# Sliding-window attention with a gated feed-forward layer: a shorter tail ahead of a branch that is jumped over

## The chip, the cores and the metric

The kernel runs on one core of a Trainium2 chip. The metric is the device time of one execution in microseconds (us); the kernel before was run three times, and the median counts. One further execution was taken with the hardware profiler, and all rows of the profile come from that one.

## What is computed

The input is one sequence of 2048 tokens with 448 features in bf16. Both halves of the layer start from the same normalised input, and their results are added to the input:

```python
xn = _layernorm(x)                                  # x is [1, 2048, 448]
# A: 16 heads of 28 features, causal window of W = 256 keys
scores = einsum("bhqd,bhkd->bhqk", q, k) * (Dh ** -0.5)
mask = (idx[:, None] - idx[None, :] >= 0) & (idx[:, None] - idx[None, :] < W)
p = softmax(where(mask, scores, -1e9))
A = (p @ v) @ wo
# B: gated feed-forward layer with 1792 hidden features
B = (gelu(xn @ w_gate) * (xn @ w_up)) @ w_down
return x + A + B
```

## The kernel before

The tokens are cut into four blocks of 512 queries (`qb`), each of four tiles of 128 rows. For each block the kernel computes scores, `Exp`, the product with the values, the gate and up projections with the Gelu, and then the down projection together with the product with `wo` (`gen_down`, L392), to which VectorE adds the input (L382, tile `res`). SyncE sends each finished tile of 128 rows to the output (L385). A plan written out by hand sets the order: the matmuls of one block are laid between the attention steps of another, so TensorE is kept busy almost without a gap. The last block has no attention step behind it, so the kernel ends with its down projection; its last tile is cut into two halves of 224 columns, and the second half (tile `pl`) is the last thing that TensorE computes.

The softmax subtracts no maximum. That is safe only while the sums of the exponentials stay in a sensible range. Near the end VectorE therefore looks at all reciprocals of these sums (`inv_all`, between `INV_LO` = 1e-18 and `INV_HI` = 1e18), reduces the answer to one integer, `flag`, and every engine loads it into a register (L889, `n_ok`). Behind the last piece of the down projection each engine compares and branches (L899): if `n_ok` is below 1, it falls through into `general_path`, which computes everything again with a maximum subtracted; otherwise it jumps over it. A hint at the head of the program tells VectorE and TensorE that this branch is likely taken; the other three engines have no hint.

Between the last residual and the branch stand three small operations that compute nothing that is used: a copy by Pool (GpSimd) of half a tile of the last `res` into `g2` (L892), a second copy by Pool of that into `g1` (L893), and VectorE's memset of one column of `g1` (L894). Since each reads or overwrites what the one ahead has written, VectorE reaches its branch only when both copies are done.

Two things about the end are not in the source and come from how the program is built. First, transfers that SyncE starts signal their landing on eight semaphores in turn, called lanes here (lane 0 to lane 7); the last output transfer is on lane 7. Second, code behind the branch counts on the same semaphore values whichever way was taken. So the side on which `general_path` is jumped over holds, for each engine, one instruction that waits until its own semaphore has its value and adds what the general path would have added; on SyncE there is one such compensating wait for each lane that the general path uses. They carry the line of the `If`, L899. Behind it stands the common end (L1020): SyncE waits for the eight lanes in order, 0 to 7, each wait paired with a second semaphore. The pair of the sixth is VectorE's count, that of the seventh TensorE's, that of the eighth ScalarE's. Then it drains, and the five engines meet in a barrier that Pool gathers, twice.

In the general path the kernel before starts 24 transfers: for each `qb` two that swap the partition halves of `xnT` into `xsw`, and one for each of the 16 tiles of the output. They use all eight lanes, three to a lane.

Of the kernel before, what the change touches and what calls it, by code (L numbers as in the profile page):

```python
# [10 lines left out]
ALU = mybir.AluOpType  # L11
AX = mybir.AxisListType
bf16 = mybir.dt.bfloat16
f32 = mybir.dt.float32
i32 = mybir.dt.int32

S, D, H, Dh, F = 2048, 448, 16, 28, 1792
P = 128
NT = S // P
NF = F // P  # L20
QB, NB = 512, 4
# [6 lines left out]
def kernel(  # L28
# [11 lines left out]
    nc = tc.nc  # L40
# [19 lines left out]
    outv = out.rearrange("b (n p) d -> p (b n) d", p=P)  # L60


    x_sb = const.tile([P, NT, D], bf16, name="x_sb")
# [36 lines left out]
    ident = const.tile([P, P], bf16, name="ident")  # L100
# [36 lines left out]
    xnT = const.tile([P, 4, S], bf16, name="xnT")  # L137
    xsw = const.tile([P, 3, 2 * QB], bf16, name="xsw")
# [205 lines left out]
    last_res = []  # L344
# [526 lines left out]
    g1 = work.tile([P, 512], f32, name="g1", tag="wc", bufs=2)  # L871
    g2 = work.tile([P, 512], f32, name="g2", tag="wb", bufs=1)
# [16 lines left out]
    n_ok = nc.values_load(flag[0:1, 0:1], min_val=0, max_val=1)  # L889
    for _ in last:  # L890
        pass
    nc.gpsimd.tensor_copy(out=g2[:, 0:D // 2], in_=last_res.pop()[:, 0:D // 2])  # L892
    nc.gpsimd.tensor_copy(out=g1[:, 0:D // 2], in_=g2[:, 0:D // 2])  # L893
    nc.vector.memset(g1[:, 0:1], 0.0)  # L894
    phase[0].close()
    fast.close()
# [7 lines left out]
def general_path(tc, locals_):  # L904

    nc = tc.nc
    L = locals_
    x_sb, xnT, qT, kT, v_sb, wd, wo, ident = (L[k] for k in ("x_sb", "xnT", "qT", "kT", "v_sb", "wd", "wo", "ident"))
    with ExitStack() as st:
        keep = st.enter_context(tc.tile_pool(name="gkeep", bufs=1))  # L910
        wk = st.enter_context(tc.tile_pool(name="gwork", bufs=2))
        ps = st.enter_context(tc.tile_pool(name="gpsum", bufs=1, space=bass.MemoryType.PSUM))
        NEG = -1e37
        mask = keep.tile([P, 3 * P], f32, name="gmask")
        nc.gpsimd.memset(mask[:, :], 0.0)
        nc.gpsimd.affine_select(out=mask[:, :], in_=mask[:, :], pattern=[[1, 3 * P]], compare_op=ALU.is_ge, fill=NEG,
                                base=-1, channel_multiplier=-1)
        nc.gpsimd.affine_select(out=mask[:, :], in_=mask[:, :], pattern=[[-1, 3 * P]], compare_op=ALU.is_ge, fill=NEG,
                                base=256, channel_multiplier=1)
        hT = keep.tile([P, NF, QB], bf16, name="ghT")  # L920
        for qb in range(NB):
            ts = slice(qb * QB, (qb + 1) * QB)
            for hi in range(2):
                nc.sync.dma_start(out=L["xsw"][64 * hi:64 * hi + 64, :, 0:QB], in_=xnT[64 - 64 * hi:P - 64 * hi, 0:3, ts])
            for f in range(NF):
                hi, p = divmod(f, 7)
                r = slice(64 * hi, 64 * hi + 64)
                pg = ps.tile([P, QB], f32, name="pg", tag="pg")
                pu = ps.tile([P, QB], f32, name="pu", tag="pu")
                for dst, w in ((pg, L["wg"]), (pu, L["wu"])):  # L930
                    for c in range(7):
                        x = xnT[r, 3, ts] if c == 6 else xnT[r, c // 2, ts] if c % 2 == hi else L["xsw"][r, c // 2, 0:QB]
                        nc.tensor.matmul(dst[:, :], lhsT=w[r, c, p * P:(p + 1) * P], rhs=x, start=(c == 0), stop=(c == 6),
                                         tile_position=(64 * hi, 0))
                ge = wk.tile([P, QB], bf16, name="gge")
                nc.scalar.activation(out=ge[:, :], in_=pg[:, :], func=ACT.Gelu_apprx_tanh)
                nc.vector.tensor_tensor(out=hT[:, f, :], in0=ge[:, :], in1=pu[:, :], op=ALU.mult)
            for g in range(4):
                pg = ps.tile([P, QB], f32, name="pg", tag="pg")
                for c in range(4):  # L940
                    n, w = (64, L["w3p"]) if c == 3 else (P, L["wqp"][:, c, :, :])
                    nc.tensor.matmul(pg[:, :], lhsT=w[0:n, 4 * g:4 * g + 4, :].rearrange("p h d -> p (h d)"), rhs=xnT[0:n, c, ts],
                                     start=(c == 0), stop=(c == 3))
                nc.vector.tensor_copy(out=qT[:, g, 0:QB], in_=pg[:, :])
            for tt in range(4):
                qt = 4 * qb + tt
                kt0 = max(0, qt - 2)
                nk = qt - kt0 + 1
                w = nk * P
                o_sb = wk.tile([P, H, 32], bf16, name="go")  # L950
                nc.vector.memset(o_sb[:, :, :], 0.0)
                for h in range(H):
                    g, r = h // 4, slice(32 * (h % 4), 32 * (h % 4) + Dh)
                    sc = ps.tile([P, 3 * P], f32, name="gsc", tag="sc")
                    nc.tensor.matmul(sc[:, 0:w], lhsT=qT[r, g, tt * P:(tt + 1) * P], rhs=kT[r, g, kt0 * P:(qt + 1) * P],
                                     start=True, stop=True, tile_position=(32 * (h % 4), 0))
                    sm = wk.tile([P, 3 * P], f32, name="gsm")
                    nc.vector.tensor_tensor(out=sm[:, 0:w], in0=sc[:, 0:w], in1=mask[:, 3 * P - w:3 * P], op=ALU.add)
                    mx = wk.tile([P, 1], f32, name="gmx")
                    nc.vector.reduce_max(out=mx[:, :], in_=sm[:, 0:w], axis=AX.X)  # L960
                    dm = wk.tile([P, 3 * P], f32, name="gdm")
                    nc.vector.tensor_scalar(out=dm[:, 0:w], in0=sm[:, 0:w], scalar1=mx[:, 0:1], scalar2=None, op0=ALU.subtract)
                    pr = wk.tile([P, 3 * P], bf16, name="gpr")
                    rs = wk.tile([P, 1], f32, name="grs")
                    nc.scalar.activation(out=pr[:, 0:w], in_=dm[:, 0:w], func=ACT.Exp, scale=SCALE, accum_out=rs[:, 0:1])
                    pT = ps.tile([P, 3, P], bf16, name="gpT", tag="pT")
                    for b in range(nk):
                        nc.tensor.transpose(out=pT[:, b, :], in_=pr[:, b * P:(b + 1) * P], identity=ident[:, :])
                    pTs = wk.tile([P, 3, P], bf16, name="gpTs")
                    nc.vector.tensor_copy(out=pTs[:, 0:nk, :], in_=pT[:, 0:nk, :])  # L970
                    ov = ps.tile([P, 32], f32, name="gov", tag="ov")
                    for b in range(nk):
                        nc.tensor.matmul(ov[:, :], lhsT=pTs[:, b, :], rhs=v_sb[:, kt0 + b, h, :], start=(b == 0), stop=(b == nk - 1))
                    ri = wk.tile([P, 1], f32, name="gri")
                    nc.vector.reciprocal(out=ri[:, :], in_=rs[:, :])
                    nc.vector.tensor_scalar(out=o_sb[:, h, 0:Dh], in0=ov[:, 0:Dh], scalar1=ri[:, 0:1], scalar2=None, op0=ALU.mult)
                for j, (t0, n) in enumerate(SLOTS):
                    c = 4 * (t0 % 7)
                    nc.vector.tensor_copy(out=o_sb[:, j:j + 4 * n - 3:4, Dh:32],
                                          in_=o_sb[:, 14 + t0 // 7, c:c + 4 * n].rearrange("p (g i) -> p g i", i=4))  # L980
                nc.vector.memset(o_sb[:, 14:16, :], 0.0)
                oT = ps.tile([P, 4, P], bf16, name="goT", tag="oT")
                for g in range(4):
                    nc.tensor.transpose(out=oT[:, g, :], in_=o_sb[:, 4 * g:4 * g + 4, :].rearrange("p h d -> p (h d)"), identity=ident[:, :])
                oTs = wk.tile([P, 4, P], bf16, name="goTs")
                nc.vector.tensor_copy(out=oTs[:, :, :], in_=oT[:, :, :])
                po = ps.tile([P, D], f32, name="gpo", tag="po")
                for g in range(4):
                    nc.tensor.matmul(po[:, :], lhsT=oTs[:, g, :], rhs=wo[:, g, :], start=(g == 0), stop=False)
                for f in range(NF):  # L990
                    nc.tensor.matmul(po[:, :], lhsT=hT[:, f, tt * P:(tt + 1) * P], rhs=wd[:, f, :], start=False, stop=(f == NF - 1))
                res = wk.tile([P, D], bf16, name="gres")
                nc.vector.tensor_tensor(out=res[:, :], in0=po[:, :], in1=x_sb[:, qt, :], op=ALU.add)
                nc.sync.dma_start(out=L["outv"][:, qt, :], in_=res[:, :])


# [28 lines left out]
```

## Time and profile before

| what | us |
|---|---|
| median of 3 runs | 214.26 |
| lowest, highest | 214.17, 214.38 |
| the profiled execution's own time | 214.34 |
| span of its instructions in the profile | 212.6 |
| the execution's time outside that span | 1.74 |

The profile is a page of views: busy time of each engine, the span in 40 slices, the DMA queues, the chain of work that ended last, and the costliest groups. Further answers of the same trace list instructions in order of time (the timeline), or all instructions of one source line. In such a list for one line a row reads: line, engine, operation, count, then the shortest, the median and the longest duration in ns, then the start of the first and of the last in us from the span's start. An engine's name with a q (SPq, DVEq) is its sequencer, which issues, waits and branches.

### The profile page before, as it was taken

What the parts mean: (1) busy time and instruction counts of PE and PEld (TensorE: products, weight loads), DVE (VectorE), ACT (ScalarE), POOL (GpSimd) and SP (SyncE); (2) the same over time, 40 slices, a digit from 0 to 9 for tenths busy, and PEclk for the clock granted to TensorE, in tenths of its full rate; (3) what the DMA queues carried; (4) which work ended last, traced back from release to release, by engine and by line L of the source; (5) the groups of instructions that cost most, each with busy time, mean ns of one, the idle gap of its engine ahead of it and who ended that gap; (6) DMA issues with size and microseconds to landing.
All of it is one profiled execution on the core that took longest, in us unless ns stands there. A gap on an engine that the chain in (4) does not pass through costs nothing.

```text
span 212.6 us, 6354 instructions
## 1 busy us (share of the span) xinstructions
PE 207.7 (98%) x2686; PEld 97.8 (46%) x2686; DVE 157.4 (74%) x355; ACT 131.6 (62%) x123; POOL 48.8 (23%) x86
## 2 busy tenths in 40 slices
PE   7999999999999999999999999999999999999993
PEld 2433444444444445444445444544444454544662
DVE  7799998999767985696537897395384798569622
ACT  4689578565777977413777787532576886656000
POOL 5287658442000220041000102023000022006001
PEclk9999999999999999999999999999999999999999
DMA  6999679978420101003421000100000001000011
GB/s 191 276 218 222 99 194 230 230 217 180 105 51 27 43 3 41 10 1 70 74 74 46 25 0 27 22 0 25 22 3 0 25 26 42 6 3 0 23 59 39
DMA packets 23993, 15.67 MB, mean 74 GB/s; under 512 B 9208, under 2 KB 23832, under 8 KB 23960
## 3 DMA queue, kind: packets, MB, share of 16 engines
q1 hardware_dynamic: 22918, 14.87, 30.4%
q8 instruction: 22, 0.36, 0.7%
q10 hardware_dynamic: 1042, 0.34, 0.7%
q14 instruction: 11, 0.09, 0.1%
HBM read 9.26 MB, written 2.41 MB: 55 GB/s over the span
## 4 chain that ended last, share of the span: by engine, by line
PE 97%; ACT 1%; issue 1%; DVE 0%; DVEq 0%; ACTq 0%
PE po L392 24%; PE gt L458 20%; PE u L458 12%; PE ue L458 8%; PE pq L334 7%; PE sc L654 6%; PE ov L626 5%; PE pv L320 4%; PE wps L150 2%; PE pq L191 2%; PE pl L392 2%; PE pv L191 1%; ACT p_sb L658 1%; PE s L191 1%; PE pk L191 1%
## 5 line engine op out<-in xcount | busy, mean ns | idle before, releaser
L658 ACT ACTIVATE p_sb<-sc 128x2048 bf16<-128x2048 f32 x39 | 73.2, 1878 | 20.5 <-PE sc L654 13.5
L498 ACT ACTIVATE p_sb<-gt 128x1024 bf16<-128x1024 f32 x28 | 28.7, 1024 | 33.7 <-PE gt L458 30.7
L593 POOL TENSOR_TENSOR oN<-oc,l 128x512 bf16<-128x512 f32 x16 | 21.6, 1356 | 119.9 <-DVE l L606 119.9
L458 PE MATMUL gt<-xnT,wg 64*128 64x512 bf16 x224 | 45.6, 376 | 0.0
L392 PE MATMUL po<-wd,hT 128*128 128x448 bf16 x210 | 43.3, 353 | 0.0
L458 PE MATMUL gt<-xsw,wg 64*128 64x512 bf16 x168 | 40.7, 376 | 0.0
L506 DVE TENSOR_TENSOR hT<-p_sb,u 128x512 bf16<-128x512 bf16 x34 | 21.9, 677 | 16.0 <-PE u L458 15.8
L574 DVE TENSOR_TENSOR p_sb<-p_sb,masks 128x256 bf16<-128x256 bf16 (+1 forms) x90 | 27.8, 363 | 7.6 <-ACT p_sb L658 7.6
L392 PEld LDWEIGHTS <-hT 128*128 128x128 bf16 x238 | 21.9, 98 | 19.4 <-issue 2.2
L458 PEld LDWEIGHTS <-wg 64*128 64x128 bf16 x392 | 19.0, 94 | 22.5 <-issue 0.2
L458 PEld LDWEIGHTS <-wu 64*128 64x128 bf16 x392 | 18.6, 94 | 22.5 <-issue 0.8
L458 PE MATMUL u<-xnT,wu 64*128 64x512 bf16 x136 | 28.1, 376 | 0.0
L458 PE MATMUL u<-xsw,wu 64*128 64x512 bf16 x102 | 24.7, 376 | 0.0
L458 PE MATMUL ue<-xnT,wu 64*128 64x512 bf16 x88 | 18.0, 377 | 0.0
L382 DVE TENSOR_TENSOR res<-po,x_sb 128x448 bf16<-128x448 f32 x15 | 9.0, 619 | 11.5 <-PE po L392 11.0
L654 PE MATMUL sc<-qT,kT 28*64 28x320 bf16 (+7 forms) x648 | 16.4, 261 | 0.1
L458 PE MATMUL ue<-xsw,wu 64*128 64x512 bf16 x66 | 16.4, 377 | 0.0
L584 POOL TENSOR_SCALAR_AFFINE_SELECT p_sb<-p_sb 128x512 bf16<-128x512 bf16 (+1 forms) x21 | 14.2, 701 | 6.6 <-ACT p_sb L658 6.5
L611 DVE TENSOR_TENSOR oc<-oc,ov 128x512 f32<-128x512 f32 x12 | 8.2, 681 | 8.7 <-ACT oc L610 8.7
L654 PEld LDWEIGHTS <-kT 28*64 28x64 bf16 (+1 forms) x648 | 7.5, 102 | 13.3 <-issue 12.0
L475 DVE CAST hT<-ue 128x512 bf16<-128x512 f32 x18 | 11.6, 680 | 1.9 <-PE ue L458 1.8
L392 PE MATMUL po<-wo,oN 128*128 128x448 bf16 x54 | 12.0, 352 | 0.0
(111 smaller groups left out, 281.8 us busy)
## 6 DMA issues: line engine op xcount, KB each, us to landing
out_dram<-res SPq DMA_DIRECT2D x15, 112.0 KB
x_sb<-in_A_x_dram SPq DMA_DIRECT2D x3, 448.0 KB
wd<-in_B_w_down_dram SPq DMA_DIRECT2D x3, 448.0 KB
xsw<-xnT SPq DMA_DIRECT2D x6, 192.0 KB
wu<-in_B_w_up_dram SPq DMA_DIRECT2D x2, 560.0 KB
wg<-in_B_w_gate_dram SPq DMA_DIRECT2D x2, 448.0 KB
wg<-in_B_w_gate_dram SPq DMA_DIRECT2D x2, 336.0 KB
wraw<-in_A_wqkv_dram SPq DMA_DIRECT2D x2, 252.0 KB
```

The source lines that it names most:

```text
L334: nc.tensor.matmul(ps, lhsT=w.rearrange("p h d -> p (h d)"), rhs=xchunk(qb, hi, c, qb * QB, QB), start=c == 0, stop=c == 6, tile_position= ...
L392: nc.tensor.matmul(po[:, 0:w], lhsT=x[:, k, tt * P:(tt + 1) * P], rhs=wt[:, k, lo:up], start=start and n == 0, stop=stop and n == len(term ...
L458: nc.tensor.matmul(ps, lhsT=w[64 * hi:64 * hi + 64, c, p * P:(p + 1) * P], rhs=xchunk(qb, hi, c, qb * QB, QB), start=c == 0, stop=c == 6, ...
L475: copy(out=hTs[qb][:, p + 7 * i, :], in_=us[i])
L498: nc.scalar.activation(out=ges[p][:, :, :], in_=gt[:, :, :], func=ACT.Gelu_apprx_tanh)
L506: nc.vector.tensor_tensor(out=hT[:, p + 7 * i, :], in0=ge[:, i, :], in1=u, op=ALU.mult)
L574: nc.vector.tensor_tensor(out=reg, in0=reg, in1=m, op=ALU.mult)
L584: nc.gpsimd.affine_select(out=reg, in_=reg, pattern=mid + [[1 if diag else -1, min(w, P)]], compare_op=ALU.is_ge, fill=0.0, base=0 if diag ...
L593: nc.gpsimd.tensor_tensor(out=oN[:, g, :], in0=oc[:, :], in1=inv, op=ALU.mult)
L626: nc.tensor.matmul(ov[half or 0][32 * j:32 * j + 32, q0:q0 + nq], lhsT=v_sb[r, kt, 4 * g + j, :], rhs=p_sb[r, j, col:col + nq], start=n == ...
L654: nc.tensor.matmul(ss[k0:k0 + nk, j, col:col + nq], lhsT=kT[r, g, kt * P + k0:kt * P + k0 + nk], rhs=qT[r, g, ring(qb).start + q0:ring(qb) ...
L658: nc.scalar.activation(out=p_sb[:, :, 0:ncol], in_=ss[:, :, 0:ncol], func=ACT.Exp, scale=SCALE)
```

## The change

The general path now makes the swapped halves by matmuls with a permutation (`gswap`), copied by VectorE into `xsw`; it adds the residual in place into `x_sb`, and sends the whole output with one transfer at its end. So it starts one transfer, on lane 0, where it started 24. Ahead of the branch one copy by Pool goes: Pool copies the half tile of the last `res` straight into `g1`, on which VectorE's memset waits as before.

```diff
-    nc.gpsimd.tensor_copy(out=g2[:, 0:D // 2], in_=last_res.pop()[:, 0:D // 2])
-    nc.gpsimd.tensor_copy(out=g1[:, 0:D // 2], in_=g2[:, 0:D // 2])
+    nc.gpsimd.tensor_copy(out=g1[:, 0:D // 2], in_=last_res.pop()[:, 0:D // 2])
     nc.vector.memset(g1[:, 0:1], 0.0)
...
         hT = keep.tile([P, NF, QB], bf16, name="ghT")
+        swap = keep.tile([P, P], bf16, name="gswap")
+        for hi in range(2):
+            nc.vector.tensor_copy(out=swap[:, 64 * hi:64 * hi + 64], in_=ident[:, 64 - 64 * hi:P - 64 * hi])
         for qb in range(NB):
             ts = slice(qb * QB, (qb + 1) * QB)
-            for hi in range(2):
-                nc.sync.dma_start(out=L["xsw"][64 * hi:64 * hi + 64, :, 0:QB], in_=xnT[64 - 64 * hi:P - 64 * hi, 0:3, ts])
+            for c in range(3):
+                pg = ps.tile([P, QB], f32, name="pg", tag="pg")
+                nc.tensor.matmul(pg[:, :], lhsT=swap[:, :], rhs=xnT[:, c, ts], start=True, stop=True)
+                nc.vector.tensor_copy(out=L["xsw"][:, c, 0:QB], in_=pg[:, :])
...
-                res = wk.tile([P, D], bf16, name="gres")
-                nc.vector.tensor_tensor(out=res[:, :], in0=po[:, :], in1=x_sb[:, qt, :], op=ALU.add)
-                nc.sync.dma_start(out=L["outv"][:, qt, :], in_=res[:, :])
+                nc.vector.tensor_tensor(out=x_sb[:, qt, :], in0=po[:, :], in1=x_sb[:, qt, :], op=ALU.add)
+        nc.sync.dma_start(out=L["outv"][:, :, :], in_=x_sb[:, :, :])
```

In the programs as built, the instructions ahead of the branch are the same on every engine but for Pool's one copy. On the side that is jumped over, SyncE's instructions go from 43 to 5, VectorE's from 1862 to 1891, TensorE's from 5796 to 5820, ScalarE's from 633 to 631; Pool keeps 12. On the side that is run, SyncE's compensating waits go from eight (lanes 0 to 7) to one (lane 0). The common end has the same instructions in the same order.

## The prediction

> **What bounds the kernel now.** I read the page first (busy time, then the chain that ended last), then the end of the chain in order of time, then the timeline of the last microseconds, and last the sequencers' rows at the branch and behind it.
>
> ```profile
> span 212.6 us, 6354 instructions
> PE 207.7 (98%) x2686; PEld 97.8 (46%) x2686; DVE 157.4 (74%) x355; ACT 131.6 (62%) x123; POOL 48.8 (23%) x86
> PE 97%; ACT 1%; issue 1%; DVE 0%; DVEq 0%; ACTq 0%
> ...
> 208.47 0.78 PE pl L392 x8
> 209.25 0.02 issue
> 209.27 0.39 DVE res L382
> 209.67 0.99 issue
> 210.66 0.08 DVEq L899
> ```
>
> The first rows are the page's: TensorE is busy for 207.7 of 212.6 us and carries 97% of the chain. The last five are the chain's end. TensorE is done at 209.25, VectorE's last residual at 209.66, and 2.9 us of the span are left in which no matmul runs. None of the change's work lies ahead of 209.66, so everything it can do to the time lies in these 2.9 us. Here is what the engines do in them:
>
> ```profile
> 209.16 0.87 SPq L385 DMA_DIRECT2D out_dram<-res  x2
> 209.27 0.39 DVE L382 TENSOR_TENSOR res<-pl,x_sb 128x224 bf16<-128x224 f32 x1
> 209.80 0.37 POOL L892 CAST g<-res 128x224 f32<-128x224 bf16 x1 [10.36 <-DVE res L382]
> 210.24 0.37 POOL L893 COPY g<-g 128x224 f32<-128x224 f32 x1
> 210.67 0.06 DVE L894 MEMSET g<- 128x1 f32 x1 [1.01 <-POOLq L899]
> ```
>
> SyncE issues the last output transfer, ending at 210.03 (209.16 plus 0.87). Beside it Pool makes its two copies, and VectorE's memset waits for them until 210.67. The view stops there, but the span runs on to 212.6. The rows by source line show by whom. First L899, the branch and the compensating waits, on SyncE: all, then the first seven waits, then the eighth alone; behind them the branch's row on VectorE.
>
> ```profile
> L899 SPq EVENT_SEMAPHORE  x8: 17/17/17, 210.6 to 211.2; - x8
> L899 SPq COMPARE_BRANCH  x1: 58/58/58, 210.1 to 210.1; - x1
> ...
> L899 SPq EVENT_SEMAPHORE  x7: 17/17/17, 210.6 to 211.1; - x7
> ...
> L899 SPq EVENT_SEMAPHORE  x1: 17/17/17, 211.2 to 211.2; - x1
> ...
> L899 DVEq COMPARE_BRANCH  x1: 84/84/84, 210.7 to 210.7; - x1
> L899 DVEq EVENT_SEMAPHORE  x1: 21/21/21, 211.3 to 211.3; - x1
> ```
>
> Then L1020, the common end: SyncE's eight waits, its drains, VectorE's drain, Pool's barrier work.
>
> ```profile
> L1020 SPq EVENT_SEMAPHORE  x8: 27/28/28, 211.3 to 211.8; - x8
> ...
> L1020 SPq DRAIN  x2: 7/10/13, 211.8 to 211.9; - x2
> ...
> L1020 DVEq DRAIN  x1: 17/17/17, 211.4 to 211.4; - x1
> ...
> L1020 POOLq EVENT_SEMAPHORE  x4: 17/17/17, 211.9 to 212.5; - x4
> ```
>
> So the tail is SyncE's: branch at 210.1, first compensating wait at 210.6, eighth at 211.2, eight waits of the common end from 211.3 to 211.8, drains to 211.9, then the barrier from 211.9 to the end. VectorE has drained at 211.4, half a microsecond ahead of SyncE. Nobody but SyncE is late, and it is late with sixteen small waits, one behind the other: seven steps in 0.6 us in the first group, 0.09 each, and seven in 0.5 us in the second, 0.07 each.
>
> **The change, part by part.** 24 transfers become one. The general path is not run, so of its transfers, copies and matmuls nothing is executed before or after: the chain's last matmul is that of L392, and every engine passes from its branch row to the compensating wait. What reaches the executed side is the number of compensating waits on SyncE. There was one for each lane used; now lane 0 alone is used, and seven of eight go. SyncE's order behind its branch at 210.1 becomes: one wait at 210.6, then the common end's eight, first at about 210.7 and, with seven steps of 0.07, eighth at about 211.2.
>
> The eighth wait is for lane 7, the last output transfer. When that lands stands in no row, but it can be bounded. It is issued by 210.03, and the eighth compensating wait, which before was the first to ask for lane 7, passes at 211.2. It comes one step of about 0.1 behind the seventh at 211.1, so it waited little or nothing for the landing. Hence the landing is no later than 211.2, and the new order asks for it at about that time too. So the eighth wait of the common end passes at 211.2 after, where it passed at 211.8 before. By the times of the rows that is 0.6; by the steps, the seven that the second group shows take 0.5, and an eighth would make it 0.57. I take 0.5 from the seven steps seen, and keep 0.6 as the upper end. If the landing were later than 211.2 the old eighth compensating wait could not have passed, so the landing alone cannot take this away; a landing that was earlier, at 211.0 say, would add up to 0.1, since then SyncE's own steps decide.
>
> [...]
>
> One copy by Pool goes: 210.24 to 210.67 is the copy with the step to the memset, 0.43 us. VectorE's memset, its branch and its compensating wait move from 210.7 and 211.3 to 210.2 and 210.9. By itself this is worth nothing while SyncE is last: VectorE had drained at 211.4 against SyncE's 211.9. With the first part it is needed. The sixth wait of the common end also asks for VectorE's count, which its compensating wait completes. With seven fewer waits SyncE asks at 210.7 + 5 x 0.07 = 211.05. Were VectorE still to arrive at 211.3, the sixth wait would stand until then, the eighth would pass at 211.3 + 2 x 0.07 = 211.45, and only 0.35 of 0.5 would be gained. At 210.9 VectorE is ahead by 0.15.
>
> What else moves costs nothing: Pool's own branch and wait come earlier and it then waits for SyncE in the barrier; TensorE and ScalarE are parked at the end of the program. Their cover is SyncE's chain, now ending at about 211.4 rather than 211.9. Pool, no longer busy up to 210.6, has its gather of the barrier free long before.
>
> The sum: 0.5 us off the span, 212.6 to 212.1. The profiled execution took 214.34, 1.74 outside the span, which nothing here touches; so 213.84 for it, and for the median of 214.26, 0.08 below the profiled execution, 213.76. That is 0.23% less. A measurement of this kernel can tell about 0.2% from no change, which is 0.43 us: the forecast clears this narrowly.
>
> **The rivals.** *VectorE becomes the last.* It is 0.15 ahead in my sum, less than the 0.6 that its branch row and its compensating wait lie apart. If that distance is not fixed but grows when the branch comes sooner, so that its count still completes at 211.3, the gain is the 0.35 above, and the time 213.91. For it speaks that SyncE, Pool and VectorE differ in how long they take from branch to wait; against it that VectorE's 0.6 is close to SyncE's 0.5.
>
> *Shorter steps without the profiler.* The steps come from the one execution that was profiled. If each takes 0.05 otherwise, eight are 0.4 and the time is 213.86. For it: the median lies 0.08 under the profiled execution; against: over a whole execution that is next to nothing. Together with the first rival this is the case between 0.2 and 0.43 us gained.
>
> *The change does nothing.* If the last arrival at the barrier is not SyncE, the time stays 214.26. The only rows that speak for it are missing ones; SyncE's second drain at 211.9 stands directly ahead of Pool's first row at 211.9.
>
> *Slower: VectorE's jump misses.* The side that VectorE jumps over grows from 1862 to 1891 instructions, so its target moves to another place in the code. What a jump costs when the code behind it is not at hand is shown by ScalarE, which has no hint:
>
> ```profile
> L899 ACTq COMPARE_BRANCH  x1: 50/50/50, 200.9 to 200.9; - x1
> L899 ACTq EVENT_SEMAPHORE  x1: 17/17/17, 203.6 to 203.6; - x1
> ```
>
> It takes 2.7 us from branch to compensating wait, where SyncE and VectorE take 0.5 and 0.6. With 2.7 VectorE's branch at 210.2 would lead to its count at 212.9; SyncE's sixth wait would stand until then, the eighth pass at 213.05 instead of 211.8, and the kernel take 1.25 us more, 215.5. It decides from 1.4 us between branch and wait on: then the sixth wait passes at 211.6, as before. Against it speaks that VectorE's target was already 1862 instructions away, and that its hint goes with the branch, not with a distance. SyncE's target comes nearer, 5 instructions for 43, so its jump has no reason to become dearer. [...]
>
> **How the numbers follow.** Forecast, a gain over 0.43: 0.62, since both bounds of the main term (0.5 and 0.6) lie above it, but the lower one by little. Gain of 0.2 to 0.43 by VectorE or by shorter steps: 0.22. Nothing: 0.07. Slower: 0.09, by VectorE's missed jump and what is like it. So faster by over 0.2% is 0.62, within 0.2% is 0.22 + 0.07 = 0.29, slower 0.09. The range goes from 213.55 (0.6 gained, and 0.1 for an earlier landing) to 214.2 (the smaller gains, and about half of the case of nothing); outside lie the slower case, the rest of nothing, and a few hundredths below: under 2 in 10.
>
> **What would show it.** Right: on SyncE one wait of L899 at about 210.6, the eight of the common end from 210.7 to about 211.2, drains to 211.3 or 211.4, a span of 212.1; VectorE's memset at 210.2 and its wait of L899 at 210.9. VectorE as the last: SyncE's sixth wait apart from the fifth, and VectorE's wait of L899 after 211.1. Wrong: a span of 212.6 with SyncE's eighth wait earlier, so that another engine is last; the eighth wait apart from the seventh and later than 211.2, which would make the landing the bound; or 2 us and more between VectorE's branch and its wait.

## The result and the profile after

The changed kernel takes 213.86 us (median of 22 executions, against 214.32 for 22 of the kernel before). The ratio is 0.998, with a 95% interval from 0.9972 to 0.9989. Run once more, beside the experiments below, it took 213.74 against 214.25, a ratio of 0.9974 (0.9965 to 0.9983). Forecast were 213.76 from 214.26, a ratio of 0.9977.

The profiled execution took 213.65 us. The first rows are its page's, the others the end of its timeline (start, duration, engine, line).

```profile
span 211.9 us, 6346 instructions
PE 207.5 (98%) x2686; PEld 97.8 (46%) x2686; DVE 157.4 (74%) x355; ACT 131.6 (62%) x123; POOL 48.3 (23%) x85
...
208.99 0.86 SPq L385 DMA_DIRECT2D out_dram<-res  x2
209.10 0.39 DVE L382 TENSOR_TENSOR res<-pl,x_sb 128x224 bf16<-128x224 f32 x1
209.63 0.37 POOL L892 CAST g<-res 128x224 f32<-128x224 bf16 x1 [10.36 <-DVE res L382]
210.06 0.06 DVE L893 MEMSET g<- 128x1 f32 x1 [0.57 <-POOLq L898]
```

This execution was already 0.17 us ahead when the last residual began (209.10, before 209.27), ahead of everything that the change touches. In the second profile of the changed kernel the residual ends at 209.64 and the span is 212.1. So profiles are compared here by the tail: from the end of the last residual to the end of the span, worked out from each trace to 0.01. It was 2.96 us before and is 2.45 after, in both profiles of the changed kernel: 0.51 less.

The rows of the two lines that make the tail, L898 (the branch) and L1023 (the common end), on SyncE and VectorE; for L1023 SyncE's first seven waits, then the eighth, its drains, and Pool's barrier work:

```profile
L898 SPq COMPARE_BRANCH  x1: 58/58/58, 209.9 to 209.9; - x1
L898 SPq EVENT_SEMAPHORE  x1: 17/17/17, 210.4 to 210.4; - x1
...
L898 DVEq COMPARE_BRANCH  x1: 84/84/84, 210.0 to 210.0; - x1
L898 DVEq EVENT_SEMAPHORE  x1: 21/21/21, 210.7 to 210.7; - x1
...
L1023 SPq EVENT_SEMAPHORE  x7: 28/28/28, 210.5 to 210.9; - x7
...
L1023 SPq EVENT_SEMAPHORE  x1: 28/28/28, 211.1 to 211.1; - x1
...
L1023 SPq DRAIN  x2: 7/10/13, 211.1 to 211.2; - x2
...
L1023 POOLq EVENT_SEMAPHORE  x4: 17/17/17, 211.2 to 211.8; - x4
```

One compensating wait is left where eight stood, and the first wait of the common end follows it at once. All eight last 28 ns, so none stood waiting for VectorE. The eighth, for lane 7, starts 0.15 us behind the seventh where the others are 0.06 to 0.07 apart: it waits 0.09 for the last output to land, at 1.56 us behind the residual's end, the same in both kernels. In the kernel before, the eighth compensating wait had done the same: it starts 0.15 behind the seventh, where the six steps ahead of it take 0.07 to 0.09, and it comes at 1.58 behind the residual's end, just as the eighth wait of the common end does now. So what the change took off the end is what SyncE still did behind the landing: the eight waits of the common end, from 1.58 to 2.09, 0.51 us.

### The profile page after: what moved, and what is told of

Read it like the earlier page. It is cut to its first block, busy times and chain, and to the rows that moved or that the text cites. A ratio compares the mean times of both kernels' runs of the same rounds, so it can differ in the third digit from the quotient of the medians.

```text
span 211.9 us, 6346 instructions
## 1 busy us (share of the span) xinstructions
PE 207.5 (98%) x2686; PEld 97.8 (46%) x2686; DVE 157.4 (74%) x355; ACT 131.6 (62%) x123; POOL 48.3 (23%) x85
## 4 chain that ended last, share of the span: by engine, by line
PE 94%; DVE 1%; ACT 1%; DMA 1%; issue 0%; DVEq 0%; ACTq 0%
PE po L392 24%; PE gt L458 20%; PE u L458 12%; PE ue L458 8%; PE pq L334 7%; PE sc L654 6%; PE ov L626 5%; PE pv L320 4%; PE pq L191 2%; PE pl L392 2%; PE pv L191 1%; DMA x_sb<-in_A_x_dram 1%; ACT p_sb L658 1%; DVE st L155 1%; PE s L191 1%; PE pk L191 1%
```

## Experiments

Each time is a median of device us beside the kernel before on the same chip, each ratio is to that, with its 95% interval; the ratio is taken over all executions, so it can differ a little from the quotient of the two medians. "Tail" is as above, from the one profile of each run. The first four kernels ran together, then the next four, then the last three.

| kernel | us | before | ratio | tail |
|---|---|---|---|---|
| the changed kernel | 213.74 | 214.25 | 0.9974 (0.9965 to 0.9983) | 2.45 |
| one transfer, two copies | 213.87 | 214.25 | 0.9984 (0.9970 to 0.9997) | 2.61 |
| 24 transfers, one copy | 214.37 | 214.25 | 1.0001 (0.9991 to 1.0012) | 2.96 |
| 8 transfers, one copy | 214.30 | 214.25 | 1.0009 (0.9996 to 1.0021) | 2.96 |
| 4 transfers, one copy | 213.93 | 214.37 | 0.9977 (0.9964 to 0.9990) | 2.59 |
| no copy, no memset | 214.66 | 214.37 | 1.0008 (0.9994 to 1.0022) | 3.18 |
| no hint for VectorE | 215.89 | 214.37 | 1.0060 (1.0040 to 1.0080) | 4.56 |
| narrow last piece | 213.95 | 214.37 | 0.9972 (0.9960 to 0.9983) | 2.66 |
| narrow, behind the last tile | 215.30 | 214.28 | 1.0042 (1.0028 to 1.0057) | 3.95 |
| VectorE's own two copies | 213.81 | 214.28 | 0.9980 (0.9970 to 0.9990) | 2.45 |
| VectorE's copy of one column | 213.71 | 214.28 | 0.9971 (0.9961 to 0.9981) | 2.45 |

**The changed kernel again.**

> The changed kernel itself, on the same chip as the others: 0.45 us under before, 2.45 us from the last residual to the end.

Tail and time came as expected: 2.45, and 0.51 under before.

**One transfer, both copies.** The first part of the change alone:

```diff
-    nc.gpsimd.tensor_copy(out=g1[:, 0:D // 2], in_=last_res.pop()[:, 0:D // 2])
+    nc.gpsimd.tensor_copy(out=g2[:, 0:D // 2], in_=last_res.pop()[:, 0:D // 2])
+    nc.gpsimd.tensor_copy(out=g1[:, 0:D // 2], in_=g2[:, 0:D // 2])
```

> One transfer in the general path, both copies by Pool kept. Theory (SyncE's waits are the tail, VectorE is next): SyncE asks for VectorE's count at about 210.8 but gets it only some 0.6 us behind VectorE's branch, so the sixth wait of the common end stands; from the end of the last residual to the end of the span 2.6 us (2.95 before, 2.45 with the whole change), the time 0.3 us under before. Rival (the second copy is of no account): all of the change's gain, 2.45 us and 0.45 under before.

The tail is 2.61, as the theory had it. The first six of SyncE's waits in the common end:

```profile
L1024 SPq EVENT_SEMAPHORE  x6: 28/28/277, 210.5 to 210.8; - x6
```

The longest, the sixth, lasts 277 ns instead of 28: it stands for VectorE's count. Of 0.51 gained with both parts, this one alone brings 0.35. By time, 0.9984 against 0.9974, the intervals overlap; the trace decides.

**24 transfers, one copy.** The second part alone, the general path as before.

```diff
-    nc.gpsimd.tensor_copy(out=g2[:, 0:D // 2], in_=last_res.pop()[:, 0:D // 2])
-    nc.gpsimd.tensor_copy(out=g1[:, 0:D // 2], in_=g2[:, 0:D // 2])
+    nc.gpsimd.tensor_copy(out=g1[:, 0:D // 2], in_=last_res.pop()[:, 0:D // 2])
```

> 24 transfers in the general path, one copy by Pool. Theory: VectorE 0.43 us earlier, SyncE as late as before, so 2.95 us from the last residual to the end and the time of before within 0.1. Rival (the chain of copies, memset and branch on VectorE sets the end): 0.43 us under before.

VectorE's compensating wait does come 0.43 earlier, 1.16 behind the residual's end against 1.59, and the tail stays 2.96. The rows of L898, SyncE's eight waits and VectorE's one:

```profile
L898 SPq EVENT_SEMAPHORE  x8: 17/17/17, 210.5 to 211.1; - x8
...
L898 DVEq EVENT_SEMAPHORE  x1: 21/21/21, 210.7 to 210.7; - x1
```

**Eight and four transfers.** The whole change, with n = 8 or 4 in

```diff
-        nc.sync.dma_start(out=L["outv"][:, :, :], in_=x_sb[:, :, :])
+        for i in range(n):
+            nc.sync.dma_start(out=L["outv"][:, i * NT // n:(i + 1) * NT // n, :], in_=x_sb[:, i * NT // n:(i + 1) * NT // n, :])
```

> The whole change, but the general path sends its output with eight transfers, one on each lane. Theory (what counts is the number of lanes that the general path uses, each a compensating wait on SyncE): eight compensating waits, 2.95 us from the last residual to the end, the time of before within 0.1. Rival (the number of transfers or the size of the code that is jumped over counts): 16 of 23 removed transfers, so 0.3 us under before.

> The whole change, but four transfers in the general path, on lanes 0 to 3. Theory (one compensating wait of 0.08 to 0.09 us each, and the landing of the last output some 0.09 us behind SyncE's own steps with one wait): three more waits are 0.26 us, of which 0.09 are hidden by the landing, so 2.62 us from the last residual to the end and 0.28 under before. Rival (the landing alone sets the end): 2.45 and 0.45 under before.

With eight the tail is that of before, 2.96, though 16 of 23 transfers are gone and all the general path's other edits are in. With four it is 2.59. The rows of L898 on SyncE, eight transfers and then four:

```profile
L898 SPq EVENT_SEMAPHORE  x8: 17/17/17, 210.5 to 211.2; - x8
```

```profile
L898 SPq EVENT_SEMAPHORE  x4: 17/17/17, 210.6 to 210.8; - x4
```

So what counts is the number of lanes that the code jumped over uses, neither its transfers nor its length. Three compensating waits more are 0.14 of tail, a little under the 0.17 expected: they take 0.24 by their own steps, and of that the landing hides 0.1.

**No delay.** Neither Pool's copy nor the memset:

```diff
-    nc.gpsimd.tensor_copy(out=g1[:, 0:D // 2], in_=last_res.pop()[:, 0:D // 2])
-    nc.vector.memset(g1[:, 0:1], 0.0)
```

> The change with neither a copy by Pool nor the memset ahead of VectorE's branch (their results are not used). Theory: VectorE reaches its wait earlier still, which is off the path, so 2.45 us from the last residual to the end and the changed kernel's time. Rival (VectorE's earlier jump, and the code fetched behind it, disturb the last output's transfer or another engine's jump): the landing comes 0.1 to 0.4 later, and the time with it.

Here the theory failed, and the rival was right, though it put the landing only 0.1 to 0.4 later: the tail is 3.18, 0.73 more than with one copy. SyncE's first seven waits of the common end, then the eighth; then VectorE's rows at the branch:

```profile
L1021 SPq EVENT_SEMAPHORE  x7: 28/28/28, 210.9 to 211.3; - x7
...
L1021 SPq EVENT_SEMAPHORE  x1: 28/28/28, 212.1 to 212.1; - x1
...
L896 DVEq COMPARE_BRANCH  x1: 84/84/84, 209.4 to 209.4; - x1
L896 DVEq EVENT_SEMAPHORE  x1: 21/21/21, 210.1 to 210.1; - x1
```

The eighth wait comes 0.89 behind the seventh: the last output lands late. The single packets in the trace, timed here from the residual's end, show where it goes. Fifteen of the transfer's sixteen landing signals come by 1.58, as ever (the last at 1.56 with the change). The sixteenth comes at 2.30. A packet of 8 KB on the queue for code starts at 0.85 and takes 0.54, up to 1.38. Of the last output's 128 data packets, which with the change all start by 1.16, eight (one sixteenth) start only when this packet ends, one behind the other from 1.38 to 1.53. They would do so if one of the 16 DMA engines that the views count had to carry both; that is the author's reading, for the trace names no engine for a packet. The queues of these microseconds (packets, MB, share of the 16 engines' time) are one for data and one for code:

```profile
q1 hardware_dynamic: 288, 0.17, 17.1%
q14 instruction: 2, 0.02, 1.7%
```

The wait behind the packet of code accounts for half of the delay: the packet that signals for those eight starts at 1.55, where the last one with the change starts at 1.18. The other half stays open: that signal lands 0.75 behind its packet where 0.38 is usual. A second packet of code runs in that time (1.77 to 2.10), but nothing shows that it is the cause.

VectorE, which branched at -0.38, had reached its compensating wait at 0.22; with the change it does so at 1.16, and the two 8 KB packets of code start at 1.53 and 1.75, behind all of the output's packets. Which engine a packet of code was fetched for, the profile does not name. The one at 1.53 starts there in the kernel before too, where VectorE's wait is 0.43 later. That the other is VectorE's follows from its moving with VectorE's jump: here, with the change and in the two runs that come next it starts 0.59 to 0.62 behind VectorE's compensating wait, and up to 0.9 behind it in the other runs with the hint.

**The delay made by VectorE itself**, by two dependent copies, and by one copy of one column:

```diff
-    nc.gpsimd.tensor_copy(out=g1[:, 0:D // 2], in_=last_res.pop()[:, 0:D // 2])
+    nc.vector.tensor_copy(out=g2[:, 0:D // 2], in_=last_res.pop()[:, 0:D // 2])
+    nc.vector.tensor_copy(out=g1[:, 0:D // 2], in_=g2[:, 0:D // 2])
```

```diff
-    nc.gpsimd.tensor_copy(out=g1[:, 0:D // 2], in_=last_res.pop()[:, 0:D // 2])
+    nc.vector.tensor_copy(out=g1[:, 0:1], in_=last_res.pop()[:, 0:1])
```

> The changed kernel with Pool's copy replaced by two copies on VectorE, each waiting for the one ahead. Theory (what matters is when VectorE jumps, since code is fetched some 0.6 us behind its jump, and that must not fall into the last output's packets): VectorE's branch 0.5 us behind the last residual as with Pool's copy, the last output lands as with the change, 2.45 us from the last residual to the end. Rival (Pool's being busy is what helps): the late landing of the run without any delay, 3.2 us.

> The changed kernel with Pool's copy replaced by a copy of one column on VectorE: VectorE's branch some 0.15 us behind the last residual, the fetch at about 1.4, behind the last output's last packet (1.2) but ahead of its landing (1.56). Theory (only packets that queue behind the fetch are held up): landing and end as with the change, 2.45 us. Rival (the fetch also holds up the landing itself): a landing 0.1 to 0.7 later, and the end with it.

Both have a tail of 2.45, with no copy by Pool at all, so it is the moment of VectorE's jump that matters and not Pool. With two copies VectorE branches 0.67 behind the residual's end. With one column VectorE branches 0.24 behind the residual's end and the first packet of code starts at 1.45, behind the output's last packet (1.18) and ahead of its landing (1.57). That is late enough: in this run the packets of code that start between the two do not hold up the landing.

**No hint.** The changed kernel without VectorE's hint:

```diff
-        if qb in (1, 3):
+        if qb == 3:
             tc.mark_branch_hint_location("general", hint="LikelyTaken",
```

> The changed kernel without the hint for VectorE's branch. Theory (a jump without a hint takes ScalarE's 2.7 us from branch to wait): VectorE's count comes at 2.7 us behind its branch, SyncE's sixth wait stands until then, some 1.8 us over the changed kernel, 1.35 over before. Rival (VectorE's code behind the branch is at hand anyway): no difference from the changed kernel.

VectorE's rows at the branch, and SyncE's first six waits of the common end:

```profile
L898 DVEq COMPARE_BRANCH  x1: 72/72/72, 210.2 to 210.2; - x1
L898 DVEq EVENT_SEMAPHORE  x1: 21/21/21, 213.2 to 213.2; - x1
...
L1023 SPq EVENT_SEMAPHORE  x6: 28/28/2227, 210.7 to 211.0; - x6
```

From branch to compensating wait VectorE takes 3.0 us, a little more than ScalarE's 2.7, and SyncE's sixth wait stands for 2.2 us. The tail is 2.11 longer than with the change (1.8 expected).

**A narrower last piece.** Since the landing now sets the end, the last tile is cut into 320 and 128 columns (Pool's copy is 128 columns too); in the second kernel the 128 columns are moreover computed wholly behind the last full tile (the part of the edit below the dots, which the first kernel does not have).

```diff
-            first, last = ((3, phase[0].pool.tile([P, 2, QB], f32, name="pl", tag="s")[:, 0, 0:D // 2], lo, lo + D // 2)
-                           for lo in (0, D // 2))
+            first, last = ((3, phase[0].pool.tile([P, 2, QB], f32, name="pl", tag="s")[:, 0, 0:up - lo], lo, up)
+                           for lo, up in ((0, 320), (320, D)))
...
-            yield from part(last, main, True)
-            yield from whole(main + late + os, 2)
-            yield from part(last, late + os, False, True)
+            yield from whole(main + late + os, 2)
+            yield from part(last, main + late + os, True, True)
```

> The changed kernel with the last tile cut into 320 and 128 columns instead of 224 and 224, and Pool's copy of 128 columns. Theory (the landing of the last output now sets the end, and it follows its issue): TensorE's part behind the last full tile is 0.3 us shorter, but SyncE is busy with the transfer ahead until 0.1 us before the old issue, so 0.1 under the changed kernel. Rival (the issue follows the residual alone): 0.25 to 0.3 under it.

> The last tile cut into 320 and 128 columns as in the run before, and all 18 matmuls of the last 128 columns put behind the last full tile, so that the transfer ahead of the last is issued well before. Theory (the landing sets the end, and it follows the issue of the last transfer, which here follows the residual alone): SyncE's eighth wait at the landing, and from the end of TensorE's last matmul to the end of the span 0.15 us less than with the whole change; the time 0.1 to 0.2 under the changed kernel. Rival (SyncE's own steps or the barrier set the end by now): no difference.

The timeline's last rows, of the first of the two kernels and then of the second:

```profile
209.37 0.28 DVE L382 TENSOR_TENSOR res<-pl,x_sb 128x128 bf16<-128x128 f32 x1
209.49 0.81 SPq L385 DMA_DIRECT2D out_dram<-res  x2
```

```profile
208.83 2.06 SPq L385 DMA_DIRECT2D out_dram<-res  x2
209.19 0.29 DVE L382 TENSOR_TENSOR res<-pl,x_sb 128x128 bf16<-128x128 f32 x1 [0.38 <-PE pl L392]
```

In the first, SyncE is still busy with the transfer ahead when the residual is done, so the last issue starts 0.27 behind the residual's end where it was 0.03. From the issue of the transfer ahead to the end it takes 2.83 us, 2.95 with the change, 0.12 less and near the 0.1 expected. But that leaves out what the cut moved: TensorE's part behind the last full tile is 0.3 us shorter, and the part ahead of it is longer by as much, so the transfer ahead itself comes later. From the start of the last residual, when TensorE is done, to the end it takes 2.94 us against 2.84, which is 0.1 longer. So the gain that was expected is not shown; the expectation counted the shorter part behind the last full tile and not the longer part ahead of it. The times (0.9972 and 0.9974) do not resolve 0.1 either way.

The second was expected to be faster still and is slower than before, 1.0042; one of its eight executions took 214.28 us, the others 215.15 to 215.68. Two issues that take 0.81 us above take 2.06 here; the last alone takes 1.39 where 0.33 is usual:

```profile
L385 SPq DMA_DIRECT2D out_dram<-res x2: 333/862/1391, 208.8 to 209.5; - x2
```

As in the run without a delay, a packet of code lies among those of the last outputs, here one that moves with TensorE's branch. TensorE branches 1.48 us ahead of the residual's end where it was 3.23 ahead, and the 16 KB packet of code that started at -1.98 now starts at -0.32 and takes 1.37 us, in the middle of the last two outputs (it starts 1.25 behind TensorE's branch in the one and 1.15 in the other). Eight of the 128 data packets of the transfer ahead start only as it ends, from 1.03 on, where the others start by 0.61, and that transfer lands at 2.21 instead of 1.16. The last lands at 3.06 instead of 1.56: its fifteen first signals come by 2.55, about 1.0 later, and so much later its issue ends (1.41 behind the residual against 0.36 with the change); the sixteenth comes 0.52 behind them, though all of its packets had started by 2.18. That last delay is not explained, and that the packet of code is the cause of the long issue was not tried by itself.

## Why the prediction was right

**The end is SyncE's waits.** Shown. With eight lanes the tail is 2.96, be it with 24 transfers or with 8; with four lanes it is 2.59, with one 2.45.

**The size, 0.5 to 0.6, taken as 0.5.** The tails give 0.51, and the bound was the one named: the eighth wait cannot pass before the landing. It stands apart from the seventh, one of the signs that the prediction gave for the landing as the bound, and SyncE now asks 0.09 too early. That the sum came out to 0.01 is in part luck. It took seven steps of 0.07 from rows that are rounded to 0.1. In the trace those seven steps take 0.44, 0.063 each, and the gain is eight of them, from the eighth compensating wait at 1.58 to the eighth of the common end at 2.09; a step that was too long made up for one too few. The prediction also read that the eighth compensating wait stood little or not at all for the landing; it stood 0.08, and without that the first group's steps are 0.08 rather than 0.09. The 0.1 that an earlier landing could have added did not come, since the landing did not move.

**Shorter steps without the profiler.** The median differences are 0.46 and 0.51, but their intervals, 0.24 to 0.60 and 0.36 to 0.75 us, do not tell 0.5 from this rival's 0.4. No run shows the 0.05 a step that it supposed: in the traces of the two kernels SyncE's steps between waits that nothing holds up are 0.06 to 0.09.

**The copy by Pool is worth nothing alone, and needed with the first part.** Shown, both halves: no gain alone (2.96), and 0.16 of tail with the first part (2.61 against 2.45). The forecast had 0.15 of 0.5. VectorE's 0.6 from branch to wait stayed the same in every run with the hint, which disposes of the rival in which it grows.

**What was overlooked.** The prediction treated the two copies as mere delay of an engine off the path, and looked at what VectorE's arrival costs if late, never at what it costs if early. Without any delay the last output lands 0.7 later. One copy was enough, so the forecast did not suffer; by the same reasoning the step to none would have been forecast as free, and it is not.

**The slower rival's price.** The jump without a hint was priced at 2.7 from ScalarE's row and cost VectorE 3.0. It did not happen in the changed kernel, whose VectorE keeps its hint and takes 0.6. That ScalarE's code was not at hand is the author's reading. The traces show packets of code beside it: in the kernel before one of 8 KB runs from 201.87 to 202.43, between ScalarE's branch at 200.93 and its compensating wait at 203.62, and the page of the run without a hint counts 12 packets on queue 14, one of the two for code, where the pages of the other kernels have 11. Which engine they were fetched for, the traces do not name.

**A detail of reading.** The prediction looked for a standing sixth wait as a gap ahead of it. In the trace these waits name two semaphores, first the lane and then the engine's count. In these runs a wait that stood for the lane started late, as the eighth did (0.15 behind the seventh with the change and 0.89 without a delay, and 28 ns long); one that stood for the count started in its place and lasted until the count was there: it is the duration, 277 or 2227 ns for 28, that tells.

## What to carry to other kernels

Code that is never run still has a price where the program rejoins: in a program built like this one, every semaphore lane that it would have used is a wait of its own at the end, a step of 0.07 to 0.09 us each on SyncE, so let a fallback path use as few lanes as it can. What such a chain costs is what of it lies behind the last arrival it waits for: here the eight waits behind the landing, 0.51. When it is shortened, look who is next: here VectorE, which with both copies held back 0.16 of the gain, and then the landing. And an engine that jumps early is not free of cost: without a delay eight of the last output's 128 packets started only when a packet of code behind VectorE's jump had ended, and the tail was 0.73 longer, half of it unexplained; keep such packets clear of them. Behind them was early enough for VectorE here, and the packet that follows TensorE's branch in the changed kernel by 1.25, done 0.67 ahead of the last residual's end, was clear of them too.

## What was not expected of the hardware

A packet of 8 KB of code that overlapped the last output's packets came with a delay of one of its sixteen landing signals from 1.56 to 2.30 us, while the other fifteen came as usual. One of 16 KB stood beside an issue of a transfer that took 1.39 us instead of 0.33. From branch to compensating wait SyncE, without a hint, takes 0.5 us and VectorE with its hint 0.6; VectorE without its hint takes 3.0, and ScalarE, which has none, 2.7 in the kernel before and 2.8 in the changed one.
